# Where twelve expert-weight transfers stand in GpSimd's stream: held back until the last attention unit's gram products

## The chip, the cores and the metric

One NeuronCore of a Trainium2 chip. The time is the device time of one execution in microseconds (us). A profile is one more execution, recorded by the hardware; its span, from the first to the last instruction, is about 2 us shorter than its time. A run counts as slow when it is more than 1.5% above the fastest run of the same kernel; ratios and their 95% intervals use fast runs alone.

## The reference, cut to what matters

```python
def reference(**kwargs):
    ...
    attn_out = _attn_ref(**attn_kwargs)   # (4, 8, 768, 48): state = w*state + k v^T, y = r (state + u k v^T)
    x = np.ascontiguousarray(attn_out.transpose(0, 2, 1, 3)).reshape(B * S, H * D)  # 3072 tokens x 384
    return _moe_ref(x=x, **moe_kwargs)

def _moe_ref(x, w_gate, w1, w2):          # 8 experts, each gets 3072 / 8 = 384 tokens, by sorted gate logits
    ...
    for e in range(E):
        mask = assigned == e
        h = np.maximum(x[mask] @ w1[e], 0.0)    # w1[e]: 384 x 1024
        out[mask] = h @ w2[e]                   # w2[e]: 1024 x 384
```

Every expert needs two weight matrices. Each is 0.786 MB as the kernel stores it (768 KB in the profile), so the experts need 16 transfers, 12.6 MB in all.

## The kernel before

The attention part runs in 24 units (6 chunks of the sequence times 4 batches). The experts follow in two passes: a first pass of 256 tokens for each expert, which needs all the weights, and a second pass of the remaining 128 tokens for each, which finds the weights in place.

The program is not written in its final order. Each operation is put in a list with its engine, an estimated duration and the operations that it comes after. A greedy list scheduler in Python (`merge`) then picks one operation after another and so fixes the order of every engine's stream, and the instructions are emitted in that order. The waits between instructions follow from the data, not from this list. The weight transfers are placed like this:

```python
LOADS = 16          # defined further up
last = NU - 1       # 23, the last unit
loaded, loads = [], []
begun = []
for e in range(E):
    users = []
    if e >= OWN:    # OWN = 4: the weights of experts 4 to 7 go into input buffers of the attention part
        ...         # users: the last readers of those buffers
    both = []
    for i, fn in enumerate(_weight_loads(nc, e, *weights[e], moe_w1, moe_w2)):
        by = [op["G", LOADS + 2 * len(loads)]] if len(loads) < 3 else []
        a = line.add("Wi", (e, i), "POOL", 800, fn, after=begun + users + by, prio=-0.9)
        begun = [a] if not loads else [a, loads[-1]]      # the next: after this issue, and the landing before it
        loads.append(line.add("Wd", (e, i), "DMA", 3500, lambda: None, after=[a], lag=1900, prio=-0.3))
        both.append(loads[-1])
    loaded.append(both)
```

`op["G", n]` are the gram products of unit n, a group of its matmuls (into `gps` in the traces). `Wi` is the issue on GpSimd, `Wd` the scheduler's model of the transfer. The issue itself is one instruction:

```python
def _weight_loads(nc, e, w1sb, w2sb, moe_w1, moe_w2):
    return [lambda: nc.gpsimd.dma_start(
                out=w1sb, in_=moe_w1[e].rearrange("(fc p) f -> p fc f", p=128)),
            lambda: nc.gpsimd.dma_start(
                out=w2sb, in_=moe_w2[e].rearrange("(fc p) d -> p fc d", p=128))]
```

GpSimd also issues, in the same in-order stream, the gathers of token rows (two for each expert of the first pass, `Fxg<-x_scratch,tok`) and the scatters of results (`out_dram<-Fos,tok`). An expert is then: gather, transpose (line 1087), first matrix (line 1117), relu, second matrix (line 1148), copy, scatter. In the traces, `w` is the buffer of experts 0 to 3, and `kr`, `vv`, `ww` are the input buffers that experts 4 to 7 use: `kr` for both matrices of experts 4 and 6, `vv` and `ww` for the first and second matrix of experts 5 and 7.

## Time and profile before

| | before |
|---|---|
| median of 3 runs | 253.95 us (252.87 to 258.76) |
| profiled execution | 266.54 us, span 264.6 us, mean granted clock 0.931 |
| TensorE busy | 215.1 us, 81% of the span |
| DMA queues of SyncE and GpSimd | 41.0% and 38.3% of 16 engines' span |

The span of the profile in 40 equal slices of 6.6 us, the digit being the busy share in tenths (9 is 90% or more):

```profile
PE   2189998799999799789689491899899997959980
...
DMA  7978789488879768999996993979999999231111
```

The seam between attention and experts is the 25th slice (158.8 to 165.4 us), where TensorE falls to 1 and the DMA engines to 3. From the 26th to the 34th slice both rows stand almost everywhere at 8 or 9: the first pass of the experts loads both fully. After it the DMA engines are nearly idle, because the second pass needs no weights.

### The profile page before, as it was taken

To read this page: it belongs to the slowest core of one execution; us is meant where nothing else is said; L and a number is where in the kernel's file an instruction comes from. 1 tells how busy PE (TensorE), PEld (TensorE's weight loads), DVE (VectorE), ACT (ScalarE), POOL (GpSimd) and SP (SyncE) were. 2 spreads that over 40 slices of the span, in tenths; PEclk is the share of its full clock that TensorE was granted. 3 is DMA by queue.
4 is the path that set the end of the run, shared out by engine and by line. 5 is a ranking of instruction groups with operands and counts; after the bars stand their busy time and mean duration, and the time that the engine had idled before them with its cause. 6 is when DMAs were issued, how large, how long until landed. Compare 5 with 4: busy or idle time off the path is not lost.

```text
span 264.6 us, 10437 instructions
## 1 busy us (share of the span) xinstructions
PE 215.1 (81%) x4469; PEld 160.1 (61%) x4469; DVE 142.9 (54%) x440; ACT 131.3 (50%) x248; POOL 148.6 (56%) x180
## 2 busy tenths in 40 slices
PE   2189998799999799789689491899899997959980
PEld 0166776577777587656477370777566765736850
DVE  6757667385677566557268760274755660114450
ACT  2156776485777577457344320374755663402300
POOL 7435685555766558747634548157764647563341
PEclk9999999999999999999779855699999999997995
DMA  7978789488879768999996993979999999231111
GB/s 149 183 148 165 143 168 223 92 173 194 160 152 214 143 131 172 193 197 168 177 228 95 206 175 80 180 165 221 167 198 213 201 191 266 86 112 67 59 69 62
DMA packets 118388, 42.24 MB, mean 160 GB/s; under 512 B 101440, under 2 KB 113728, under 8 KB 118336
## 3 DMA queue, kind: packets, MB, share of 16 engines
q1 hardware_dynamic: 104128, 21.84, 41.0%
q0 software_dynamic: 14208, 19.66, 38.3%
q8 instruction: 37, 0.61, 0.9%
q14 instruction: 15, 0.12, 0.2%
HBM read 46.61 MB, written 7.47 MB: 204 GB/s over the span
## 4 chain that ended last, share of the span: by engine, by line
PE 68%; DVE 8%; DMA 8%; issue 7%; another core or an unknown queue 3%; ACT 3%; POOL 2%; POOLq 0%; DVEq 0%
PE yps L320 11%; PE tps L478 8%; PE gps L320 7%; PE tps L320 7%; PE cps L320 7%; PE gps L1117 6%; PE gps L1148 6%; PE cps L1117 6%; PE cps L1148 5%; DMA vv<-in_moe_w_dram 4%; DMA ww<-in_w_dram 3%; PE tps L590 2%; PE tps L1087 1%; DVE Dohl L870 1%
## 5 line engine op out<-in xcount | busy, mean ns | idle before, releaser
L466 POOL TENSOR_TENSOR mm<-diag,dd 128x512 f32<-128x512 f32 x24 | 25.1, 1048 | 57.5 <-DVE dd L461 31.1
L484 ACT COPY krT<-tps 112x512 f32<-112x512 f32 x48 | 28.1, 586 | 23.4 <-PE tps L478 20.4
L1168 POOL DMA_INDIRECT out_dram<-Fos,tok x24 | 24.1, 1003 | 24.7 <-DVE Fos L1158 13.7
L1076 POOL DMA_INDIRECT Fxg<-x_scratch,tok x24 | 23.5, 977 | 20.3 <-PE tps L1087 11.1
L557 DVE COPY_PREDICATED mm<-mask,gps 128x256 f32<-128x256 uint8 x48 | 18.7, 442 | 27.9 <-PE gps L320 16.7
L320 PE MATMUL cps<-ww,negut 128*128 128x384 f32 x48 | 23.3, 569 | 12.1 <-issue 6.3
L478 PE MATMUL tps<-ident,krs 128*112 128x128 f32 x192 | 31.5, 290 | 0.6 <-DVE Dboth L710 0.6
L478 PEld LDWEIGHTS tps<-ident,krs 128*112 128x112 f32 x192 | 22.7, 140 | 10.9 <-issue 6.2
L320 PE MATMUL yps<-mm,vv 64*48 64x64 f32 x768 | 19.9, 232 | 9.0 <-DVE mm L557 6.0
L457 POOL TENSOR_TENSOR rku<-rku,u_bc 128x384 f32<-128x384 f32 x24 | 24.0, 1000 | 2.6 <-DMA u_bc<-in_u_dram 2.6
L453 POOL TENSOR_TENSOR rku<-kr 128x384 f32<-128x384 f32 x24 | 24.1, 1003 | 2.2 <-DMA kr<-in_r_dram 2.2
L320 PEld LDWEIGHTS yps<-mm,vv 64*48 64x48 f32 x768 | 14.6, 125 | 17.5 <-DVE mm L557 10.7
L1148 PEld LDWEIGHTS <-Fhs 128*128 128x128 bf16 x192 | 17.8, 99 | 11.9 <-issue 2.8
L578 ACT COPY xf<-yps 128x512 f32<-128x512 f32 x24 | 14.0, 582 | 22.1 <-PE yps L320 22.1
L447 DVE TENSOR_TENSOR krs<-kr,cps 128x768 f32<-128x768 f32 x24 | 22.7, 945 | 1.7 <-ACT cps L442 1.6
L320 PE MATMUL yps<-krT,sm 48*48 48x64 f32 x384 | 21.6, 229 | 1.1 <-issue 1.1
L442 ACT ACTIVATE cps<-cps 128x768 f32<-128x768 f32 x24 | 19.3, 804 | 5.0 <-DVE cps L438 5.0
L320 PE MATMUL yps<-krT,st 48*48 48x64 f32 x384 | 21.3, 228 | 0.3 <-issue 0.3
L1134 ACT ACTIVATE Fhs<-gps 128x512 bf16<-128x512 f32 x20 | 12.0, 598 | 15.5 <-PE gps L1117 9.4
L320 PE MATMUL gps<-krT 48*64 48x64 f32 x768 | 18.4, 227 | 1.0 <-issue 1.0
L1134 ACT ACTIVATE Fhs<-cps 128x512 bf16<-128x512 f32 x20 | 11.8, 598 | 13.8 <-PE cps L1117 10.3
L1117 PEld LDWEIGHTS <-w 128*128 128x128 bf16 x192 | 15.1, 100 | 5.8 <-issue 4.1
(200 smaller groups left out, 464.5 us busy)
## 6 DMA issues: line engine op xcount, KB each, us to landing
w<-in_moe_w_dram POOLq DMA_DIRECT2D x8, 768.0 KB
ww<-in_w_dram SPq DMA_DIRECT2D x24, 192.0 KB, 3.9
kr<-in_k_dram SPq DMA_DIRECT2D x24, 192.0 KB, 4.0
kr<-in_r_dram SPq DMA_DIRECT2D x24, 192.0 KB, 4.2
vv<-in_v_dram SPq DMA_DIRECT2D x24, 192.0 KB, 4.1
kr<-in_moe_w_dram POOLq DMA_DIRECT2D x4, 768.0 KB
x_scratch<-row SPq DMA_DIRECT2D x7, 384.0 KB, 4.9
vv<-in_moe_w_dram POOLq DMA_DIRECT2D x2, 768.0 KB
```

What stands on the lines that cost most here:

```text
L320: ln.last = nc.tensor.matmul(*a, **kw)
L447: fn=lambda u=u, kr=kr, b=b: nc.vector.tensor_tensor(out=KR[slot(("kr", u))][:, :, :, :D], in0=kr[:, b].rearrange("t x (h d) -> t x h d", ...
L453: fn=lambda u=u, kr=kr, b=b: nc.gpsimd.tensor_tensor(out=P[slot(("p", u))], in0=kr[:, b, 0, :], in1=kr[:, b, 1, :], op=ALU.mult))
L457: fn=lambda u=u: nc.gpsimd.tensor_tensor(out=P[slot(("p", u))], in0=P[slot(("p", u))], in1=u_bc, op=ALU.mult))
L466: fn=lambda u=u: nc.gpsimd.tensor_tensor(out=M[slot(("m", u))], in0=_free(diag, [0, 2], [0, NPAIR], [1, 64]), in1=_free(Dg[slot(("dg", u)) ...
L478: ln.last = nc.tensor.transpose(t[:112, at:at + 128], pair_of(s[:, x], j), ident)
L484: nc.scalar.copy(out=KRT[slot(("krt", u))][:112, 2 * half:2 * half + 2].rearrange("p j x t -> p (j x t)"), in_=Tps[slot(("t", u, half))][: ...
L1076: got = nc.gpsimd.indirect_dma_start(out=self.xg[slot[xg[1]]], out_offset=None, in_=self.x_dram, in_offset=bass.IndirectOffsetOnAxis(ap=to ...
L1117: nc.tensor.matmul(self.bank("B", b[1])[:, i * size:(i + 1) * size], lhsT=w1sb[:, k, f8 * 128:(f8 + 1) * 128], rhs=xv()[:, k], start=(k == ...
L1134: nc.scalar.activation(out=to, in_=of, func=AF.Relu)
L1148: nc.tensor.matmul(self.bank("B", b[1])[:, :DX], lhsT=hv()[:, f8, h * 128:(h + 1) * 128], rhs=w2sb[:, f8, :], start=(f8 == 0), stop=(f8 == ...
L1168: put = nc.gpsimd.indirect_dma_start(out=self.out, out_offset=bass.IndirectOffsetOnAxis(ap=tok[:, j:j + 1], axis=0), in_=self.os[slot[o[1] ...
```

## The change

Its intent is to keep the weight traffic out of the last attention units: before, transfers 4 and 5 went out while the last unit was still at work. Now every transfer but the fourth (number 3) waits in the scheduler's list for some unit's gram products, and from number 4 on for those of the last unit.

```diff
-                by = [op["G", LOADS + 2 * len(loads)]] if len(loads) < 3 else []
+
+                n = len(loads)
+                by = [op["G", LOADS + 2 * n if n < 3 else last]] if n != 3 else []
```

## The prediction

> **What bounds the kernel now.** The program has two halves: 24 attention units on all engines, then eight experts, each needing two weight transfers (one for its first matrix, one for its second; 16 in all, numbered 0 to 15 here). I read the page's DMA queues first, then GpSimd's timeline, because every weight transfer is issued from GpSimd's in-order stream.
>
> ```profile
> q1 hardware_dynamic: 104128, 21.84, 41.0%
> q0 software_dynamic: 14208, 19.66, 38.3%
> q8 instruction: 37, 0.61, 0.9%
> ```
>
> The columns are packets, MB, share of 16 engines. The weights are in q0: 16 x 0.786 MB = 12.6 of its 19.66 MB; the rest are the gathers of token rows (24 x 0.098 MB) and the scatters of results (24 x 0.197 MB).
>
> GpSimd's timeline (start, duration, instruction, idle before it); w, kr, vv and ww are the buffers that weights go to:
>
> ```profile
> 140.18 0.94 POOL L1026 DMA_DIRECT2D w<-in_moe_w_dram  x1
> ...
> 147.12 0.80 POOL L1024 DMA_DIRECT2D w<-in_moe_w_dram  x1
> 147.93 0.92 POOL L1026 DMA_DIRECT2D w<-in_moe_w_dram  x1
> ...
> 156.33 1.05 POOL L1076 DMA_INDIRECT Fxg<-x_scratch,tok  x1 [0.32 <-DVE tok L890]
> ...
> 163.68 0.83 POOL L1024 DMA_DIRECT2D w<-in_moe_w_dram  x1
> 164.48 0.97 POOL L1026 DMA_DIRECT2D w<-in_moe_w_dram  x1
> ...
> 208.45 0.81 POOL L1024 DMA_DIRECT2D vv<-in_moe_w_dram  x1
> ...
> 212.80 0.95 POOL L1026 DMA_DIRECT2D ww<-in_moe_w_dram  x1
> ```
>
> Transfer 3 goes out at 140.18, 4 and 5 at 147.12 and 147.93, then the first six gathers from 156.33 (when VectorE has made the token list), then 6 and 7, and the last two, for expert 7, at 208.45 and 212.80. Durations here are only the issue.
>
> Windows of the trace (columns: length, busy time and count of PE, weight load, VectorE, ScalarE, GpSimd, granted clock, DMA share, GB/s written):
>
> ```profile
> 147.00:158.00 11.00, 7.11 (x145) 5.53 (x146) 9.23 (x40) 2.54 (x5) 4.25 (x6) 0.62 1.12 191
> 158.00:165.00 7.00, 1.69 (x17) 0.93 (x14) 0.00 (x0) 0.00 (x0) 5.78 (x7) 0.50 0.32 87
> 165.00:175.00 10.00, 8.99 (x123) 6.63 (x124) 3.01 (x15) 4.43 (x10) 2.47 (x3) 0.74 1.12 204
> 175.00:187.00 12.00, 10.89 (x94) 8.03 (x93) 7.85 (x34) 7.46 (x16) 8.64 (x9) 1.00 0.72 153
> 187.00:219.00 32.00, 31.07 (x269) 21.66 (x267) 19.21 (x95) 18.90 (x38) 18.39 (x20) 1.00 1.11 204
> ```
>
> From 187 to 219 the transfers are saturated (share 1.11) and PE is busy 31.07 of 32 us: both are at their limit. Weights arrive just in time, with nothing to spare. The chain of waits, and PE's timeline at the same place, say who is last:
>
> ```profile
> 157.21 7.93 another core or an unknown queue
> ...
> 208.45 11.26 DMA vv<-in_moe_w_dram
> ```
>
> ```profile
> 217.62 0.49 PE L1148 MATMUL cps<-kr,Fhs 128*128 128x384 bf16 x2
> 219.76 1.48 PE L1117 MATMUL gps<-Fxe,vv 128*128 128x256 bf16 x12 [1.65 <-DMA vv<-in_moe_w_dram]
> ```
>
> Transfer 14 is issued at 208.45 and PE is released at 219.76: about 11 us for one 0.786 MB transfer, because it queues behind others. PE itself idles only 1.65 us, since it had other work. A caution: the profiled execution took 266.54 us, the three timed ones 252.87 to 258.76. The unexplained 7.93 us piece at 157.21 is a candidate for what timed runs lack; if so PE reaches expert 7 earlier there, and weights are more of a limit than the trace shows.
>
> **What the Trainium skill says.** "DMA: Bandwidth & Descriptors", section "Issuing engines are not separate DMA queues": transfers from SP, ScalarE and GpSimd all run on the same 16 DMA engines and interleave. The trace agrees: q0 and q1 together hold 79.3% of the 16 engines. The same page, "Anatomy of one DMA — SWDGE (gpsimd) path": a semaphore is waited for on the issuing sequencer, and the DMA engines only consume their queues. That fits transfer 14: issued at once, landed 11 us later behind a backlog. "Runtime: NRT & Kernel Launch", section "Instruction fetch mechanics": a sequencer fetches 16 KiB blocks over its own DMA queue. The trace agrees on the size (q8: 0.61 MB / 37 = 16.5 KB); this matters for a rival below.
>
> **The change part by part.** The new condition sits in the list that orders operations before the program is emitted; the transfer itself is the same instruction. So it adds no instruction and no wait of its own: it moves transfers 4 to 15 to later places in GpSimd's stream, behind the last unit's gram products. Comparing the two built programs shows the moves. GpSimd has 227 rows in both.
>
> 1. Transfers 4 and 5 move from before the last unit's mask product to behind the first six gathers: from 147 to about 163.7 us, the place that 6 and 7 had. The gathers do not come earlier by this: they wait for the token list (0.32 us idle, VectorE L890).
> 2. All later ones move back about two places, some more. Before, transfer 14 stood behind the scatters of expert 3; now it stands behind the first scatter of expert 5, and 15 behind the second. Those scatters cannot issue until expert 5 is computed.
> 3. TensorE's order is rearranged around it: the rest of expert 6, and the first group of the second pass (a smaller block of 128 tokens per expert), move ahead of expert 7.
>
> The price. Between 147 and 158 the DMA engines wrote 191 GB/s with PE and VectorE busy on other things; 1.57 MB of it was transfers 4 and 5. That capacity is now unused, and the bytes are added to the stage that is already saturated. Before, from 163.7 on: 10 weights (7.86 MB), 10 gathers of the first pass (0.98 MB) and 12 scatters of experts 0 to 5 (2.36 MB), 11.2 MB; at 204 GB/s that is 55 us, to 218.7, plus about 2 us to be seen, which agrees with PE starting on the last weights about 224. After: 1.57 MB more, 1.57 / 0.204 = **7.7 us later**. The slack at 175 to 187 (share 0.72) does not take it up: it comes from GpSimd waiting for transposes before it may issue, and transfer 6 now stands where 8 stood.
>
> Item 2 adds: 14 cannot start before expert 5's first output, and expert 5 is itself late, so I put +1.5 us on it. Item 3 takes back work done while PE waits: expert 6's remaining second-matrix products (6 + 8 at 0.163 us, 2.3 us of it before expert 7 now), of which some already overlapped; and about 0.7 us of second-pass work. I count -2.5 us. Gain at the front: the first gather lands sooner, being alone in the queue, perhaps 1 us, but PE needs it only after the last unit's output, so 0 to -0.5 us.
>
> Sum: 7.7 + 1.5 - 2.5 - 0.3 = +6.4 us; 253.95 + 6.4 = 260.4.
>
> **The rivals.**
> A. The transfers are hidden anyway. If PE, not DMA, sets the pace of the experts in timed runs, part of the 7.7 us goes into slack. For: PE idle at expert 7 is only 1.65 us, and PE is busy 31.07 of 32. Against: PE already waits 1.65 us for transfer 14, so there is no slack left behind it; any delay of the weights is felt at once, unless the gap at 175 to 187 fills. Time: 254 to 257.
> B. The held-back traffic was what stalled PE at 157.21 (7.93 us), perhaps through its instruction fetches, and the change removes it. For: it falls on the last gram products, which the new condition names, right after 4 and 5 moved. Against: in 158 to 165 the DMA share is 0.32, so the queue was not full; what runs there is six gathers and two weight issues back to back on GpSimd (5.78 of 7 us busy), and exactly the same sequence stands there after the change. Time if true and present in timed runs: 248 to 253.
> C. GpSimd's in-order stream becomes the bound: each late weight delays an expert, whose scatter delays the next weight issue, and the lag compounds over experts 4 to 7. For: item 2. Against: the order interleaves them so that usually two transfers are in flight. Time: 264 to 268.
>
> **Range and chances.** The central sum gives 260.4. A and B pull down, C up; the 2% limits are at 248.9 and 259.0. The sum lies only 1.4 us above the upper limit, and run-to-run spread is large (252.87 to 258.76), so "within 2%" keeps a third. Range 254.3 to 266.0. Faster 0.07, within 0.32, slower 0.61.
>
> **What would show it.** In the changed profile: weight issues 4 and 5 after six gathers, near 164 us; a DMA share clearly under 1 in the window between the token list's making and the gathers, and saturation reaching to about 230; PE idle before experts 4 to 7 with the weights' DMA as releaser, several us in all instead of 1.65; a chain with a longer DMA piece at expert 7. If the 7.93 us piece still stands at the last gram products, B is wrong; if it is gone and timed runs are faster, B is right. The prediction is wrong if PE waits no longer for weights than now, which would mean the stage was not saturated in the runs that count.

## More of the kernel before

Before ran more often in each set of experiments than any other kernel (7 or 11 runs against 4 or 6), so its fastest run lies lower and the ratios come out a little high. The ratio of the medians of all runs is given beside them where this matters.

## The result

| | before | after |
|---|---|---|
| median of 4 runs each, same chip | 254.27 us (252.87 to 258.76) | 264.11 us (262.86 to 266.12) |
| profiled span, granted clock | 264.6 us, 0.931 | 263.0 us, 0.941 |

The ratio is 1.0413, with an interval of 1.0314 to 1.0513. Here and below a ratio is the mean time of one kernel's fast runs over that of the other's of the same rounds, so it is not quite the ratio of the medians (264.11 / 254.27 = 1.039). A later set of five rounds on another chip gave 264.65 us against 255.57, ratio 1.0481. The change costs 4 to 5%, some 9 to 12 us (by medians of all runs 1.039 and 1.036).

The two profiled spans are nearly equal, and a reader who compares only these would conclude the opposite. The profiled execution of before took 266.54 us, which none of its timed runs did. So a second profile of before was taken (experiment `again`: span 252.5 us). It is the proper partner of the profile after, and is used as such below.

The 40 slices of the profile after:

```profile
PE   2089998798999888979798677999997857789980
...
DMA  7969799578868878998996902899999999932121
```

The 24th and 25th slices (151 to 164 us) now read 0 and 2 in the DMA row: hardly anything moves. In return the 9s go on to the 35th slice, up to 230 us. TensorE reads 7, 8, 5, 7, 7 in slices 31 to 35, where it had 9, 9, 9, 7, 9 before.

GpSimd's timeline of after (start, duration, instruction, idle before it), at the places that the prediction showed of before:

```profile
141.97 0.93 POOL L1026 DMA_DIRECT2D w<-in_moe_w_dram  x1
...
157.49 1.06 POOL L1076 DMA_INDIRECT Fxg<-x_scratch,tok  x1 [0.32 <-DVE tok L890]
...
164.84 0.82 POOL L1024 DMA_DIRECT2D w<-in_moe_w_dram  x1
165.64 0.97 POOL L1026 DMA_DIRECT2D w<-in_moe_w_dram  x1
...
217.15 0.82 POOL L1024 DMA_DIRECT2D vv<-in_moe_w_dram  x1
...
220.58 0.95 POOL L1026 DMA_DIRECT2D ww<-in_moe_w_dram  x1
```

Between 141.97 and 164.84 no weights are issued. Transfer 14 goes out at 217.15; in the second profile of before it was at 202.82. The durations of about 0.9 us are only the issue. The Trainium skill says so too: "Perfetto Trace Analysis", section "DMA Instruction — SWDGE (GPSIMD)", puts the profiler's end of such an instruction at the end of descriptor generation, not of the data movement. The trace agrees: the issue takes 0.82 us, and the two transfers to `vv` landed a median of 9.6 us after their issue.

The same windows as in the prediction (length, busy time and count of PE, weight load, VectorE, ScalarE, GpSimd, granted clock, DMA share, GB/s written), first of after:

```profile
147.00:158.00 11.00, 7.46 (x162) 5.66 (x162) 8.76 (x41) 3.11 (x6) 3.31 (x5) 0.78 0.31 49
158.00:165.00 7.00, 5.37 (x131) 4.45 (x134) 1.03 (x3) 2.27 (x6) 5.47 (x7) 0.50 0.26 73
165.00:175.00 10.00, 10.00 (x80) 6.97 (x73) 4.98 (x24) 5.34 (x12) 5.81 (x7) 0.74 1.00 176
175.00:187.00 12.00, 11.72 (x93) 8.33 (x92) 8.22 (x36) 7.53 (x15) 9.19 (x11) 1.00 1.13 228
187.00:219.00 32.00, 26.29 (x232) 17.78 (x230) 16.14 (x82) 14.99 (x31) 17.83 (x19) 1.00 1.15 215
```

and of before in its second profile (`again`):

```profile
147.00:158.00 11.00, 6.81 (x158) 5.32 (x158) 9.09 (x40) 2.42 (x5) 4.73 (x6) 0.76 1.17 199
158.00:165.00 7.00, 5.28 (x147) 4.09 (x140) 1.64 (x5) 2.32 (x6) 5.30 (x6) 0.74 0.59 117
165.00:175.00 10.00, 9.76 (x85) 6.88 (x79) 6.02 (x28) 6.52 (x14) 7.47 (x9) 0.93 0.94 164
175.00:187.00 12.00, 11.96 (x93) 8.34 (x91) 7.13 (x32) 7.71 (x16) 7.84 (x9) 1.00 1.11 227
187.00:219.00 32.00, 30.92 (x271) 21.73 (x270) 15.93 (x81) 18.50 (x37) 20.61 (x22) 1.00 1.17 241
```

Two columns matter. In the first two rows the last column falls from 199 and 117 to 49 and 73. Multiply each GB/s by its window and add up the first four rows: before had written 199 x 11 + 117 x 7 + 164 x 10 + 227 x 12 = 7372 KB by 187 us, after only 49 x 11 + 73 x 7 + 176 x 10 + 228 x 12 = 5546 KB. The difference is 1.83 MB, a little more than the two transfers that the change moved (1.57 MB). In the last row TensorE's busy time falls from 30.92 to 26.29 of 32 us, at the same full clock. Whether the missing bytes are paid for there is what the experiments test. The share in the second and third rows of before also shows that the gap which the prediction saw at 175 to 187 us (0.72) belonged to the first profile only; here it is 1.11.

TensorE's waits from 164 to 240 us in the profile after (line waited for: us in all, times, longest):

```profile
PE cps L1148 <- DMA kr<-in_moe_w_dram: 2.6, 2, 1.6
PE cps L1117 <- DMA kr<-in_moe_w_dram: 1.6, 1, 1.6
PE gps L1148 <- ACT Fxe L1101: 1.3, 1, 1.3
PE gps L1117 <- DMA vv<-in_moe_w_dram: 1.2, 1, 1.2
PE tps L1087 <- DMA Fxg<-x_scratch,tok: 1.1, 1, 1.1
PE cps L1117 <- DMA vv<-in_moe_w_dram: 0.9, 1, 0.9
```

Before had, in the same stretch of its second profile, one wait for weights:

```profile
PE gps L1117 <- DMA vv<-in_moe_w_dram: 1.1, 1, 1.1
```

The weights of experts 4 to 7 are now late one after another: 2.6 + 1.6 + 1.2 + 0.9 = 6.3 us. The 1.3 us put down to ScalarE's `Fxe` is probably a sixth late transfer (the four sums hold five waits): at the same instruction group a second profile of this kernel has the transfer to `ww` as the releaser, with 1.4 us. The chain of waits of after has this piece near the end of the first pass:

```profile
221.84 9.77 DMA Fxg<-x_scratch,tok
```

It is a gather of the second pass, issued right behind transfers 14 and 15 and landing 9.77 us later, so even what comes after the weights is late; that fits their backlog.

How much of the loss is waiting? Take the stage from TensorE's first matmul of expert 0 to the end of the span, and add up its windows. The line of sums of before (`again`), from 167.0 us to the end:

```profile
sum 85.50, PE 75.81 PEld 55.52 DVE 40.12 ACT 39.48 POOL 49.89; mean PE 15.16 PEld 11.10 DVE 8.02 ACT 7.90 POOL 9.98
```

and of after, from 166.3 us:

```profile
sum 96.70, PE 78.51 PEld 56.66 DVE 40.08 ACT 39.77 POOL 51.29; mean PE 13.08 PEld 9.44 DVE 6.68 ACT 6.63 POOL 8.55
```

The stage is 11.2 us longer. TensorE's idle time in it goes from 85.50 - 75.81 = 9.7 us to 96.70 - 78.51 = 18.2 us, 8.5 us more. The other 2.7 us is busy time. In the first 14 us of this stage the granted clock was 0.86 in the profile after and 1.00 in `again`, which is worth an estimated 14 x 0.14 = 2.0 us. Whether that belongs to the change isn't shown. All nine profiles of after and its variants have 0.86 to 0.97 in these 14 us. Of the five of before and its variants, four have 1.00 (two_late, which is slow, among them), but ahead2 has 0.86 (the variants are told below).

### The profile page after: what moved, and what is told of

It is laid out like the page before. It is cut to its first block, busy times and chain, and to the rows that moved or that the text cites. A ratio compares the mean times of both kernels' runs of the same rounds, so it can differ in the third digit from the quotient of the medians.

```text
span 263.0 us, 10431 instructions
## 1 busy us (share of the span) xinstructions
PE 214.5 (82%) x4469; PEld 159.9 (61%) x4469; DVE 143.3 (54%) x440; ACT 131.9 (50%) x248; POOL 148.6 (56%) x180
## 5 line engine op out<-in xcount | busy, mean ns | idle before, releaser
L484 ACT COPY krT<-tps 112x512 f32<-112x512 f32 x48 | 28.1, 586 | 26.9 <-PE tps L478 23.8
L320 PE MATMUL cps<-ww,negut 128*128 128x384 f32 x48 | 24.2, 588 | 11.9 <-issue 7.0
L1148 PEld LDWEIGHTS <-Fhs 128*128 128x128 bf16 x192 | 17.5, 98 | 14.2 <-issue 4.5
L320 PE MATMUL yps<-krT,st 48*48 48x64 f32 x384 | 21.9, 232 | 0.0
L320 PEld LDWEIGHTS yps<-krT,sm 48*48 48x48 f32 x384 | 15.5, 128 | 4.7 <-issue 3.7
L1117 PEld LDWEIGHTS <-w 128*128 128x128 bf16 x192 | 15.7, 102 | 3.5 <-issue 1.1
L320 PE MATMUL gps<-krT 48*64 48x64 f32 x768 | 17.0, 228 | 0.8 <-issue 0.8
## 6 DMA issues: line engine op xcount, KB each, us to landing
kr<-in_moe_w_dram POOLq DMA_DIRECT2D x4, 768.0 KB, 12.5
```

Source lines behind the costliest of these rows:

```text
L320: ln.last = nc.tensor.matmul(*a, **kw)
L484: nc.scalar.copy(out=KRT[slot(("krt", u))][:112, 2 * half:2 * half + 2].rearrange("p j x t -> p (j x t)"), in_=Tps[slot(("t", u, half))][: ...
L1117: nc.tensor.matmul(self.bank("B", b[1])[:, i * size:(i + 1) * size], lhsT=w1sb[:, k, f8 * 128:(f8 + 1) * 128], rhs=xv()[:, k], start=(k == ...
L1148: nc.tensor.matmul(self.bank("B", b[1])[:, :DX], lhsT=hv()[:, f8, h * 128:(h + 1) * 128], rhs=w2sb[:, f8, :], start=(f8 == 0), stop=(f8 == ...
```

## The experiments

The theory after the result was this. TensorE uses up one expert in about 7 us (in `again`, experts 4, 5 and 6 begin at 191.4, 198.4 and 205.3 us). The DMA engines need longer for one: by the sizes in the prediction it takes 1.57 MB of weights, 0.20 MB of gathers and 0.39 MB of scatters, 2.16 MB; at the 215 GB/s of after's window from 187 to 219 us that is an estimated 10.0 us (9.0 us at the 241 GB/s of `again`). So by this theory the kernel lives on a stock of weights that it has brought in ahead, and the change makes the stock two transfers smaller. Rivals: the first profile's oddities (prediction's B); the loss lies only in transfers 4 and 5 themselves; it lies in where the later ones stand; it lies in TensorE's rearranged order.

Most experiments take the order that the scheduler has found and shift single operations before it is emitted:

```diff
-        for _, o in done:
+        order = [o for _, o in done]
+        loads_at = {o.u: o for o in order if o.name == "Wi"}
+        seq = [loads_at[i // 2, i % 2] for i in range(16)]     # transfers 0 to 15
+        places = [order.index(o) for o in seq]
+        # ... the shift of this experiment ...
+        for o in order:
             o.fn()
```

Twelve runs were made, two of them of the unchanged kernels, on three chips; each ratio is against before on the same chip. Of one set, one run of before took 391.44 us and was left out as slow.

### again: before, unchanged

No edit.

> The kernel before, unchanged, for a second trace. The first profiled execution took 266.54 us, the timed ones 252.87 to 258.76. If the 7.93 us piece at the last gram products and the stretch at 233 to 238 where PE trickled belong to that one execution, this profile has a span near 252 us without them, and PE idles longer for the last experts' weights than the 1.65 us of the first trace (2 to 5 us). If they belong to the kernel, the span is near 264 again. Timed: ratio 1.00 (0.99 to 1.01).

It took 255.86 us (253.88 to 259.41), ratio 1.0014 (0.9692 to 1.0336), span 252.5 us, clock 0.951. The 7.93 us piece of the chain is not there, and TensorE is busy 5.28 us between 158 and 165 us instead of 1.69. That stall was in the one execution only. The change cannot have removed it, and it is no part of what is compared. One part of the expectation failed: TensorE waits 1.1 us for the last expert's weights, not 2 to 5, so before is less held by weights than its first profile showed (1.65 us), not more.

### changed: the change, five rounds

No edit to after.

> The changed kernel itself on this chip, for comparison with the three below: ratio to before 1.03 to 1.05 (both theories).

264.65 us (263.44 to 268.49) against 255.57 (250.45 to 258.86), ratio 1.0481 (1.0376 to 1.0585), clock 0.944. The loss repeats on another chip.

### two_late: before, with only transfers 4 and 5 late

```diff
+        move((2, 0), "F256g", 5)        # transfer 4 right behind the sixth gather
+        order.remove(loads_at[2, 1])
+        order.insert(order.index(loads_at[2, 0]) + 1, loads_at[2, 1])   # and 5 behind it
```

> The kernel before with only transfers 4 and 5 moved behind the sixth gather; every other operation keeps its place in every engine's stream. Theory 1 (the two transfers lose an idle stretch of the DMA engines, and their bytes lengthen a stage that is saturated): 259 to 262 us. Theory 2 (what costs is where the later transfers 8 to 15 stand in GpSimd's stream, behind scatters of later experts, and the rearranged order of the other engines; the bytes themselves fit): 253 to 256 us.

265.1 us (261.09 to 267.54), ratio 1.0418 (1.0255 to 1.0582). The median is above theory 1's 259 to 262 us and far from theory 2's. TensorE's order and all other places are those of before, and the whole loss is there. But it comes by another wait. The chain of waits of this kernel:

```profile
167.09 17.59 DMA Fxg<-x_scratch,tok
```

and TensorE's longest wait:

```profile
PE tps L1087 <- DMA Fxg<-x_scratch,tok: 6.6, 1, 6.6
```

Four weight transfers go out in a row here, from 163.39 to 165.85 us. The 0.098 MB gather behind them, issued at 167.09, was there only 17.59 us later. Four transfers are 3.15 MB; at the 222 GB/s written from 175 to 187 us that is an estimated 14.2 us of backlog. TensorE ran out of tokens instead of weights. The Trainium skill, "DMA: Bandwidth & Descriptors", section "Two DMAs through the same engine are not ordered", says that in one queue of one DMA engine descriptors start in order. The wait fits this; no run here shows single descriptors.

### two_early: after, with transfers 4 and 5 given back their early places

```diff
+        move((2, 0), "DG", last, True)   # in front of the last unit's mask product, as before
+        move((2, 1), "DG", last, True)
```

> The changed kernel with transfers 4 and 5 put back before the last mask product, where the kernel before has them; all else stays in the changed order, transfers 6 to 15 too. Theory 1: 254 to 257 us. Theory 2: 260 to 264 us. Both in part: 257 to 260.

264.85 us (263.2 to 270.59), ratio 1.0325 (1.0164 to 1.0487). Giving back the two transfers that the change is named for gives nothing that can be told from the change's own loss. One window shows why:

```profile
165.00:175.00 10.00, 9.72 (x91) 7.12 (x92) 4.06 (x19) 5.73 (x13) 4.24 (x6) 0.73 0.28 83
```

The hole in the DMA share has moved from 147 to 165 us to here (0.28): transfers 4 and 5 are early, but 6 is still where the change put it. By 187 us this kernel had written 5636 KB, hardly more than after (5546). So the loss doesn't lie in transfers 4 and 5 themselves. The time is the one that theory 2 forecast (260 to 264 us): by this run alone the late places of the other transfers could be the cause as well. It takes `half`, below, to part the two.

### six_early: after, with transfers 4 to 7 early

```diff
+        order[places[4]], order[places[5]] = seq[6], seq[7]   # 6 and 7 at the places of 4 and 5
+        del order[places[7]], order[places[6]]
+        i = next(i for i, x in enumerate(order) if (x.name, x.u) == ("DG", last))
+        order[i:i] = seq[4:6]
```

> The changed kernel with 4 and 5 back before the last mask product and 6 and 7 at the places of 4 and 5; 8 to 15 where the change has them. Theory H: the hole moves on again, to about 175-187, because 8 waits in GpSimd's stream for expert 1's scatter: 259 to 264 us, DMA share under 0.7 in some stretch of 8 us between 172 and 190. If the two early transfers were what mattered: 254 to 257 us.

263.28 us (257.82 to 267.15); too few fast runs for a ratio, and the profile is slow. Where its hole lies:

```profile
175.00:187.00 12.00, 11.66 (x92) 8.27 (x91) 8.22 (x36) 7.48 (x15) 7.68 (x8) 1.00 0.65 170
```

The hole has moved on once more, to 175 to 187 us. TensorE still waits for `kr` (1.4 + 1.4 us), `ww` (1.1) and `vv` (1.0 + 0.8).

### after_up: after, with all of transfers 4 to 15 two places earlier

```diff
+        for i in range(6, 16):
+            order[places[i - 2]] = seq[i]
+        del order[places[15]], order[places[14]]
+        i = next(i for i, x in enumerate(order) if (x.name, x.u) == ("DG", last))
+        order[i:i] = seq[4:6]
```

> The changed kernel's order of everything but the weight transfers; transfers 4 and 5 stand before the last mask product again and 6 to 15 two places earlier each. Theory H (what counts is the idle the DMA engines have before the last transfer; with two_early the hole only moved from 147-165 to 165-175): no hole is left, so 253 to 257 us. Theory R (the changed order of TensorE, ScalarE and the scatters costs of itself): 259 to 264 us.

263.91 us (261.76 to 266.47), ratio 1.036 (0.9977 to 1.0744): the interval is wide, because before had only two fast runs in this set. All four runs lie above all seven of before (252.37 to 259.51), so theory H's 253 to 257 us was missed and theory R's 259 to 264 us was met. Its profile (fast, span 261.4 us) has no wait for weights at all, and yet it is long. One wait stands out in TensorE's timeline:

```profile
223.24 0.34 PE L1087 MATMUL tps<-ident_bf,Fxg 128*128 128x128 bf16 x3 [2.74 <-DMA Fxg<-x_scratch,tok]
```

The change had put the first group of the second pass ahead of expert 7's first matrix. With the weights in time, TensorE stands at that group and waits for its tokens, whose gather was issued at 215.22 us behind the last two weights, while expert 7 could have gone on.

### up_swap and swap: that group moved behind expert 7's first matrix

up_swap is after_up, swap is after, both with

```diff
+        i = next(i for i, x in enumerate(order) if (x.name, x.u) == ("F256u", (7, 7)))
+        later = [x for x in order[:i] if x.name[:4] == "F128" and x.engine in ("PE", "ACT", "DVE")]
+        order[i + 1:i + 1] = later
+        for x in later:
+            del order[order.index(x)]
```

> after_up (weights early, all else in the changed order) with the second pass's work that stands before expert 7's first matrix (a transpose of a gathered tile, its copy, nine matmuls) moved behind it on TensorE and the copying engine. after_up's chain ended in a 7.97 us piece on that gather. Theory G (TensorE's in-order wait for the second pass's gather, which queues behind the last weights, is what the changed order costs): 255 to 259 us, PE's wait for gathers under 1 us before expert 7. Theory R in another form (the order of experts without overlap of one's second with the next one's first matrix): still 261 to 265 us.

> The changed kernel with the same move on TensorE, weights left late. If late weights hold expert 7 anyway: within 1.5 us of the changed kernel, and PE's wait moves from the gather to the weights. If the gather is a cost of its own on top: 3 to 5 us less than the changed kernel.

up_swap: 257.45 us (254.5 to 261.1), ratio 1.0152 (1.0051 to 1.0252), against changed in the same rounds 1.0481. Weights two places earlier and that group behind expert 7 together win back two thirds of the loss. Its profile has no wait for weights and none for a gather.

swap: 263.9 us (262.15 to 265.35), ratio 1.0429 (1.0333 to 1.0525), which can't be told from changed. With the weights late, it doesn't matter where the group stands. Its profile shows why: expert 7's first matrix waits 2.9 us for `vv` (0.9 in after) and expert 5's second matrix 2.2 us for `ww`; what the group covered before is waited out now.

### half: after, with transfers 8 to 15 of half the size

Same instruction order on every engine, same places of issue, wrong result (relative error 0.71): the missing half of the weights of experts 4 to 7 is replaced by the half that is there.

```diff
+    if e >= OWN:
+        w1sb, w1, w2sb, w2 = w1sb[:, :, :F // 2], w1[:, :, :F // 2], w2sb[:, :4], w2[:, :4]
...
-   lhsT=w1sb[:, k, f8 * 128:(f8 + 1) * 128]
+   lhsT=w1sb[:, k, f8 % m * 128:(f8 % m + 1) * 128]      # m = 4 if e >= OWN else 8
...
-   rhs=w2sb[:, f8, :]
+   rhs=w2sb[:, f8 % m, :]
```

> The changed kernel with transfers 8 to 15 cut to half their bytes (experts 4 to 7 use the loaded half twice: the result is wrong on purpose, instructions and order are the same). If the saturated DMA engines are what makes weights late: 3.1 MB less at about 0.22 MB per us is 14 us less queue, so PE's waits for weights vanish, 253 to 257 us. If it is the place of the issues in GpSimd's stream alone: 260 to 264 us.

257.32 us (256.1 to 258.27), ratio 1.0113 (0.9921 to 1.0306), clock 0.939. The median is 0.3 us above the expected range, and by medians of all runs the ratio is 1.002. No wait for weights is left, and the waits for gathers add up to 1.0 us (line 1089 is line 1087 of the other kernels):

```profile
PE tps L1089 <- DMA Fxg<-x_scratch,tok: 1.0, 2, 0.6
```

Over the stage from 167.7 us to the end:

```profile
sum 88.60, PE 77.99 PEld 56.80 DVE 39.80 ACT 39.80 POOL 51.41; mean PE 13.00 PEld 9.47 DVE 6.63 ACT 6.63 POOL 8.57
```

TensorE is idle for 88.60 - 77.99 = 10.6 us, against 18.2 in after and 9.7 in `again`. The stock at 187 us is after's (5562 KB against 5546), but the rest of the demand is smaller, and nearly the whole loss is gone. So the late places of the issues alone don't cost it. What this run can't part is the shorter queue from the shorter transfer: both make weights land sooner (a median of 6.7 us after the issue to `kr`, against 12.5 in after). Transfer 14 goes out at 214.18 us here, 3 us sooner than in after although its place in the stream is the same: expert 5, whose scatter stands in front of it, is no longer late. It is still 11.4 us later than in `again` (202.82), and costs next to nothing.

### behind2: before, with the transfers late but TensorE's old order

```diff
+        for i in range(4, 14):
+            order[places[i + 2]] = seq[i]
+        del order[places[5]], order[places[4]]
+        for i, j in ((14, 10), (15, 11)):      # behind the two scatters of expert 5
+            g = next(i for i, x in enumerate(order) if (x.name, x.u) == ("F256s", j))
+            order.insert(g + 1, seq[i])
```

> The kernel before with every transfer from 4 on two places later in GpSimd's stream, 14 and 15 behind the two scatters of expert 5; the other engines keep the order of before. Theory H: as slow as the changed kernel, 260 to 266 us, with a hole at 147-158 and PE waiting for weights of experts 4 to 7 for 6 us or more in all. Theory R: 254 to 257 us, since nothing is rearranged.

281.36 us (275.23 to 286.4); only one fast run (275.23), so no ratio, and its profile is slow. Both expectations were missed, theory H's 260 to 266 us by 9 us even in the fastest run. That fastest run is still 6.7 us above the slowest run of the change in any set (268.49). TensorE's waits in it:

```profile
PE gps L1117 <- DMA kr<-in_moe_w_dram: 11.7, 2, 6.9
PE gps L1117 <- DMA vv<-in_moe_w_dram: 8.6, 1, 8.6
```

In the old order, an expert's first matrix is interleaved ahead of the second matrix of the one before. A late first matrix therefore holds up the finished expert's output too, and with it the scatter, and with that the next issues of weights. The profile shows one such case: GpSimd stood idle for 7.96 us before expert 3's scatter at 206.11 us, and transfer 11 behind it went out at 208.97, against 190.25 in `again` (part of that by its later place). In the order of the change an expert's second matrix follows its own first, which should keep the lateness from feeding on itself like this; no run moves that alone.

### hold5: half the dose

```diff
-                by = [op["G", LOADS + 2 * n if n < 3 else last]] if n != 3 else []
+                by = [op["G", LOADS + 2 * n if n < 3 else last]] if n not in (3, 4) else []
```

> The same change from the sixth transfer on: transfer 4 keeps its early place (147 us), 5 is held back behind the gathers and the list is ordered anew. Half the hole, so by the sum of bytes about half the loss: 257 to 261 us. If the loss comes from the first late transfer of all, as for two_early, 262 to 265.

260.96 us (257.2 to 263.15), ratio 1.0254 (1.0125 to 1.0383), beside 1.0481 for the change in the same rounds. Its profile is slow. With transfer 4 free again, about half the loss is left, just inside what the sum of bytes had (257 to 261 us).

### ahead2: before, with a larger stock

```diff
+        for i in range(8, 16):
+            order[places[i - 2]] = seq[i]
+        # ... the two last places go; 6 and 7 behind the second and the fourth gather
```

> The kernel before with transfers 6 to 15 each two places earlier in GpSimd's stream: 6 behind the second gather, 7 behind the fourth, 8 at the place of 6, and so on. It uses the stretch at 158 to 165 where the DMA share is 0.32. If the kernel before is held by the weights in timed runs (theory 1), 249 to 253 us; if PE alone sets its pace, 253 to 256; if the gathers behind the two transfers come too late for PE, 255 to 258.

256.04 us (254.38 to 257.47), ratio 1.001 (0.9883 to 1.0137). Its 1.1 us wait at expert 7 is gone and nothing is gained that these rounds can see. Before has as large a stock as it needs, and no version better than both kernels was found.

### All together

The stock is what was written from 147 to 187 us, worked out from each kernel's windows as above. The stage runs from TensorE's first matmul of expert 0 to the end of the span.

| kernel | stock, KB | stage, us | ratio to before | profile's state |
|---|---|---|---|---|
| ahead2 | 7777 | 85.7 | 1.001 | fast |
| again (before) | 7372 | 85.5 | 1.001 | fast |
| after_up | 7307 | 92.3 | 1.036, wide | fast |
| up_swap | 6897 | 87.4 | 1.015 | slow |
| six_early | 6522 | 93.4 | none | slow |
| hold5 | 6306 | 91.8 | 1.025 | slow |
| swap | 5838 | 96.6 | 1.043 | fast |
| changed | 5813 | 94.1 | 1.048 | fast |
| two_late | 5647 | 94.8 | 1.042 | fast |
| two_early | 5636 | 96.0 | 1.033 | fast |
| after | 5546 | 96.7 | 1.041 | fast |
| half | 5562 | 88.6 | 1.011 | fast |
| behind2 | 5718 | 113.4 | none | slow |

Leave out the last two: half has a smaller demand, and behind2 has all the later transfers late in TensorE's old order. Then the three fast profiles of about 7.3 MB and more are the ones without a late weight (but for 1.1 us in before), and every kernel between 5.5 and 5.9 MB lies at 1.03 to 1.05, whichever of the transfers were the late ones. This order was seen after the runs, not predicted. What speaks for cause and not only for company is `half`, which keeps the small stock and takes away the demand. The first profile of before (slow) is not in the table: it would stand at 6586 KB and 93.2 us with only 1.6 us of waits for weights. A single execution's stage can thus be off by several us.

## Why the prediction was right

The time on record was 260.4 us, and 264.11 came: inside the range, slower by over 2% as held most likely, but low by 3.7 us.

- **What bounds the kernel, and the mechanism: right.** The weights became late, TensorE waits for them at experts 4 to 7 (6.3 us in the profile, against 1.1), and the DMA engines stay saturated to 230 us. The places of the issues came as worked out: 4 and 5 at 164.84 and 165.64 us (predicted 163.7), 14 behind the first scatter of expert 5.
- **Item 1, the bytes, +7.7 us: right in kind and in size.** The stock is short by 1.83 MB; at 215 GB/s that is 8.5 us. In the second profile of changed it is short by 7372 - 5813 = 1559 KB, 7.3 us. But the prediction tied the cost to transfers 4 and 5. two_early and six_early show that it belongs to no particular transfer: an early place given back to some only moves the hole along to the next.
- **"The slack at 175 to 187 does not take it up": right for a wrong reason.** The second profile of before has no slack there. It was a mark of the one odd execution. The check that the last weights come at 218.7 us, "which agrees with PE starting on the last weights about 224", is none: TensorE came to them at 224.66 us without waiting for them, and two of the 12 scatters counted were issued at 218.72 and 220.03 us, behind the last transfer (212.80).
- **Item 2, the place of 14 and 15, +1.5 us: can't be separated.** Transfer 14 is issued 14.3 us later than in `again`. Part of that is the place and part the lateness of expert 5 itself. half puts a number to the second: with the place unchanged, 14 went out 3 us sooner.
- **Item 3, "I count -2.5 us": in doubt, and not settled.** The rearrangement does shorten what comes after expert 7, from 31.4 to 28.1 us between the end of its second matrix and the end of the span. But the work brought forward waits for its own tokens, whose gathers queue behind the last weights (1.1 us in after, 2.7 in changed). Moving the second pass's group back cost nothing (swap 1.0429, changed 1.0481), so that part of the credit, about 0.7 us, is worth about nothing in time. The larger part, expert 6's second matrix (up to 2.3 us), was never moved alone. Without the whole credit the prediction's own sum is 7.7 + 1.5 - 0.3 = 8.9 us, and the medians differ by 9.8; that it fits is no proof.
- **Item 3 as a safeguard: not seen at all.** behind2 points the other way. With the old order similar lateness costs 18 us even in the fastest run (275.23 against a median of 256.93 for before), so as a whole the rearrangement may save more than the 2.5 us. Which term made the sum 3.7 us low stays open.
- **The gain at the front, -0.3 us: too small to test.** Expert 0 begins at 166.3 us against 167.0, and over all the profiles it lies anywhere from 164.4 to 171.9.
- **Rival A** (hidden anyway) is out: the kernel was 10 us slower. **Rival B** (the 7.93 us stall) fell with `again`. **Rival C** (compounding, 264 to 268) has the right size and half the mechanism: the experts of after begin 11.4, 9.5 and 9.7 us apart (196.1, 207.5, 217.1 and 226.8 us). That is near the DMA engines' pace of an estimated 10.0 us, a steady loss at each expert, where behind2 compounds. One sign announced didn't come: the chain of after has no longer piece for expert 7's weights, but 9.77 us for the gather behind them.

**What stays open.** up_swap has enough stock and no wait for weights or gathers, and is still 0.5 to 2.5% slower than before; half likewise has 1.1%, though its interval holds 1. By medians of all runs, slow ones too, they are at 1.007 and 1.002, so the remainder may be smaller than it looks. It is hardly waiting: in the stage TensorE is idle for 9.2 us in up_swap and 10.6 in half (9.7 in `again`), and busy for 78.16 and 77.99 us (75.81). In both, TensorE keeps the changed order of the experts' matrices. Whether this order costs the remainder was not tested by itself. The profile of half has the clock at 0.91 in the first 14 us of the stage, as against 1.00 in `again`, so part of the difference in stage (88.6 against 85.5 us) may be the clock. Whether the middle of the table (six_early, hold5) would hold in fast profiles is open too.

## What to carry to other kernels

In this kernel a stage needs more bytes for each step than the DMA engines bring in the time of the step (an expert: about 7 us of TensorE, an estimated 9 to 10 us of transfers). What counted then was how much was in place when the stage began. So where a stage looks like this, count the bytes written up to that moment, and don't clear away traffic ahead of it because the engines look busy with other things. The Trainium skill's rule "Issue the DMA early, do compute, wait on its semaphore late" ("DMA: Bandwidth & Descriptors", section "Rules for kernel authors") holds here with a number: two transfers fewer ahead cost 4 to 5% of the whole kernel. The page's reason is that the fixed setup cost overlaps; here it was the transfer itself and its queue. A small, urgent transfer behind large ones in the same stream can pay for their backlog (17.59 us for a gather in two_late), and a profile of a single execution should be taken again before anything in it is explained.

## What the Trainium skill lacked or had wrong

- "DMA: Bandwidth & Descriptors", section "Anatomy of one DMA — SWDGE (gpsimd) path": its fit for one DMA, 2.0 us + bytes / 436 GB/s, gives an estimated 3.8 us for 0.786 MB. In the profile after, the weight transfers landed a median of 8.5 us (`w`), 9.6 us (`vv`) and 12.5 us (`kr`) after their issue, which fits queueing. The page gives the fit for a DMA by itself and no way to estimate the backlog; backlog over the GB/s written in that window came within 3.4 us here (14.2 us estimated, 17.59 measured for a gather).
- The same page, section "Two DMAs through the same engine are not ordered": it warns about correctness, but not about time. A 0.098 MB gather issued 1.24 us after the last of four 0.786 MB transfers on the same stream took 17.59 us, and stopped TensorE for 6.6 us.
- No page that we read tells that one execution may contain stalls that others of the same program don't have: in the first profile of before TensorE was busy 1.69 of 7 us from 158 to 165 us and the chain has 7.93 us for which the profile names no releaser, in the second 5.28 us and no such piece. Its cause stays unknown.
